# Which engine evicts the first transposed tile: a fixed choice in a planned FFT-convolution and GLU kernel

## The chip, the cores and the metric

The kernel runs on one core of one Trainium2 chip. The metric is the device time of one execution in microseconds; lower is better. Engines are named as in the profile: PE is TensorE, DVE is VectorE, ACT is ScalarE, POOL is GpSimd, SP is SyncE.

## The reference

The kernel computes the output and nine gradients of one block: a layer normalization, a gated long convolution of H3 type on one side, a gated linear unit on the other, and a residual sum. S is 2048, D is 512, F is 1376, everything is bf16.

```python
xn = _layernorm(x)                              # x = A_q
k_shift = sum(k_pad[:, t:t+S] * shift_k[:, 3-t] for t in range(4))
kv = k_shift * v
y = irfft(rfft(kv, 2*S) * rfft(ssm_k, 2*S))[:S] + kv * ssm_D
s = xn * y
g, u = xn @ w_gate, xn @ w_up
z = (sigmoid(g) * u) @ w_down
out = x + s * silu(z)
# returned: out, and the gradients for A_q, A_k, A_v, A_shift_k, A_ssm_k, A_ssm_D,
# B_w_gate, B_w_up, B_w_down against grad_out
```

## The kernel before

**Tiles.** The 2048 rows of the sequence are cut into 16 tiles of 128 rows. They are taken in the order `SEQ`, which begins with 15, 13, 11, 9, 7, 5, 0, 1, 2; `POS[i]` is the place of tile i in that order, so `POS[15]` is 0. The 512 channels are cut into four groups `cg` of 128 for the convolution.

**First part, to some 160 us.** Four streams are woven together. `strG` makes the forward half of the gated unit for nine tiles: `f_gen(i)` multiplies the transposed normalized tile `xnT` with `w_gate` and `w_up` in three chunks (`FBS`, of 4, 4 and 3 blocks of 128 columns), ScalarE makes the sigmoid of one half of the result, and VectorE multiplies the other half by it. `strK`, `strV` and `strX` make the long convolution as a transform by matmuls: `k_t` transposes the kernel of a channel group, `step1` is the first transform stage, `flip` a transpose, `step3` the second stage, `inv3` and `inv1` the way back. `strV` also has the four-tap shift as multiplies and adds of 128x2048 on VectorE. `gen_ci` transposes constants for the way back, and `gen_fft_consts` makes the transform's constants with sines on ScalarE right at the start. `w_gen`, early in the second part, transposes the last pieces of the weights.

**Second part.** From there `stepB` makes the down projection and the gradients tile by tile, `dW` the weight gradients, `frontC` and `backC` the gradients of the convolution.

**The transposed tile.** `f_ln` normalizes tile i into `xnA[:, i]`. `f_xt(i)` makes `xnT`. For the first four places of `SEQ`, and for places 9 to 11, it makes four TensorE transposes into a PSUM bank and evicts them with one copy of 128x512 in bf16; for the others a DMA transpose does it. `f_xt(15)` is called on its own ahead of the streams; `f_xt` of the next tile is called inside `f_gen`.

**What sets the order.** Nothing is issued where it is written. Every call is recorded by `Rec.add`, with its dependencies, and `Rec.order` then lays out all recorded operations on the five engines, from its own costs and due times: at each step it takes, over the engines, the operation that can start earliest, and among those that are ready on an engine the one that was recorded first. `Rec.emit` issues the result, which is why nearly all instructions of the profile have the line number 523. An operation waits on the chip only for what it needs, but each engine takes its instructions strictly in the planned order.

An eviction made with `nc.evac` is recorded with two alternatives, and the planner decides:

```python
def evac(self, dst, src, n):
    op = self.add([("scalar", "copy", (dst, src), {}), ("vector", "tensor_copy", (dst, src), {})])
    op.bias = 0.3 if esize(src.ap.dtype) == 2 else 0
```

In `order` such operations stand in the list `either`. VectorE gets one only when ScalarE would be late with it by more than 0.4 or 1.6 us of the planner's time, and bf16 evictions carry a bias of 0.3 towards VectorE. An operation recorded for one engine alone goes into that engine's own list.

PSUM has eight banks. A tile of PSUM is given its bank by the planner too. Results that need two banks (`mm2`: `f_gen`, `step1`, `step3`, `inv3`, `inv1` in the first part) take one of four pairs, of which the third is shared with `acc` (banks 4 and 5) and the fourth with `tr` (banks 6 and 7, where every transpose goes):

```python
KINDS = {"mm2": [(0, 1), (2, 3), (4, 5), (6, 7)], "mm2c": [(0, 1), (2, 3)], "mm1": [(0,), (1,), (2,), (3,)],
         "acc": [(4,), (5,)], "tr": [(6,), (7,)]}
```

DMAs are issued from SP (weights, k, v, half swaps of the transform, DMA transposes) and from POOL (x tiles after the third, stores to the scratch tensors `hF_d`, `sF_d`, `KK_d`, `ksh_d`).

Of the kernel before, what the change touches and what calls it, by code (L numbers as in the profile page):

```python
# [37 lines left out]
POS = {i: n for n, i in enumerate(SEQ)}  # L38
# [599 lines left out]
def kernel_impl(ctx, tc, A_q, A_k, A_v, A_shift_k, A_ssm_k, A_ssm_D, B_x, B_w_gate, B_w_up, B_w_down,  # L638
                grad_out, out_0, out_1, out_2, out_3, out_4, out_5, out_6, out_7, out_8, out_9):
    nc = tc.nc  # L640
# [24 lines left out]
    def ps_tr(shape, dt=bf16, name=None):  # L665
        return nc.ps("tr", shape, dt)
# [25 lines left out]
    T = [dict() for _ in range(NJ)]  # L692
# [31 lines left out]
    def f_xt(i):  # L724
        if POS[i] > 3 and not 8 < POS[i] < 12:
            T[i]["xnT"] = xnT_r.next()
            nc.sync.dma_start_transpose(T[i]["xnT"], xnA[:, i, :])
            return
        pt = ps_tr([4, 128], name="ps_xnT")
        for db in range(4):  # L730
            nc.tensor.transpose(pt[:, db, :], xnA[:, i, db * 128:(db + 1) * 128], ident)
        T[i]["xnT"] = xnT_r.next()
        nc.evac(T[i]["xnT"], pt[:], 512)

    def f_gen(i):
        xnT = T[i]["xnT"]
# [7 lines left out]
        for pi, (f0, nb) in enumerate(FBS):  # L744
            if PS["wide"]:
                ps = ps_mm([2, 4, 128], name="psGU")
                pg, pu = ps[:, 0], ps[:, 1]
            else:
                pg, pu = ps_mm([4, 128], name="psG")[:], ps_mm([4, 128], name="psU")[:]
            for pt_, w in ((pg, wg), (pu, wu)):  # L750
                for b in range(nb):
                    for db in range(4):
                        nc.tensor.matmul(pt_[:, b, :], w[:, db, (f0 + b) * 128:(f0 + b + 1) * 128], xnT[:, db, :],
                                         start=(db == 0), stop=(db == 3))
            nc.scalar.activation(sigT[:, f0:f0 + nb, :], pg[:, 0:nb, :], ACT.Sigmoid)
            if uT is None:
                nc.vector.tensor_tensor(hT[:, f0:f0 + nb, :], pu[:, 0:nb, :], sigT[:, f0:f0 + nb, :], ALU.mult)
            else:
                nc.evac(uT[:, f0:f0 + nb, :], pu[:, 0:nb, :], nb * 128)
            if pi == 1 and n + 2 < NJ:  # L760
                f_ln(SEQ[n + 2])
            if pi == (2 if n == 0 else 0) and n + 1 < NJ:
                f_xt(SEQ[n + 1])
            yield nb * 1024
# [101 lines left out]
    for db in range(4):  # L866
        pb = ps_acc([512])
        nc.tensor.matmul(pb[:], ones1, skr[:, db * 512:(db + 1) * 512], start=True, stop=True)
        nc.scalar.copy(skb[:, :, db * 128:(db + 1) * 128], pb[:].rearrange("p (d t) -> p t d", t=4))
    next(consts)  # L870
    f_xt(SEQ[0])
    f_ln(SEQ[1])
    next(consts)
# [668 lines left out]
```

## Time and profile before

| What | us |
|---|---|
| median of 6 runs | 515.98 |
| lowest and highest | 514.41, 519.02 |
| the profiled execution | 516.2 |
| its span, first to last instruction | 514.4 |
| PE busy | 494.6 (96%) |
| DVE busy | 387.1 (75%) |
| ACT busy | 349.8 (68%) |
| POOL busy | 129.3 (25%) |

A row of a timeline gives start, length, engine, line, operation, output and input, and how many instructions were merged into it; brackets hold the idle time before it and what ended that. A windows row gives, for a stretch, the busy time and the number of instructions of each engine, the granted TensorE clock, the busy share of the DMA engines and what they moved. A group row gives busy time, mean length in ns, and idle time with its releasers.

### The profile page before, as it was taken

How to read it: one execution, taken by the hardware profiler on the slowest of the kernel's cores; microseconds unless marked ns; L12 is line 12 of the kernel's file. 1: busy time of each engine (PE TensorE's matmuls, PEld its weight loads, DVE VectorE, ACT ScalarE, POOL GpSimd, SP SyncE). 2: the span in 40 equal slices, each digit the busy share in tenths (PEclk: the TensorE clock that was granted, in tenths of full speed). 3: DMA queues.
4: the chain of work that ended last, by engine and by line, in shares of the span. 5: the costliest groups of instructions: out<-in, count | busy, mean ns of one | idle time of the engine just before them, and what ended most of it. 6: DMA issues, size and time to landing. Idle time of an engine off the chain costs nothing.

```text
span 514.4 us, 13559 instructions
## 1 busy us (share of the span) xinstructions
PE 494.6 (96%) x5437; PEld 352.3 (68%) x5437; DVE 387.1 (75%) x772; ACT 349.8 (68%) x467; POOL 129.3 (25%) x251
## 2 busy tenths in 40 slices
PE   5699999999999999999999999999999999999997
PEld 3688897889886676666666556644675665866644
DVE  7688999986758789867779988426759859698440
ACT  6799999998874565465545546426878988886611
POOL 7243526255413333414153311000010010010000
PEclk9999999999999999999999999999999999999999
DMA  8989997599997555737499946989799699999973
GB/s 208 314 213 293 314 316 241 171 294 241 255 216 200 159 154 163 201 110 192 119 252 228 278 153 173 217 256 249 170 236 253 171 263 309 207 237 243 199 218 97
DMA packets 181392, 112.92 MB, mean 220 GB/s; under 512 B 131441, under 2 KB 165777, under 8 KB 181074
## 3 DMA queue, kind: packets, MB, share of 16 engines
q1 hardware_dynamic: 169376, 77.78, 64.2%
q0 software_dynamic: 11424, 34.29, 20.8%
q8 instruction: 42, 0.69, 0.6%
q14 instruction: 20, 0.16, 0.1%
q10 hardware_dynamic: 530, 0.01, 0.1%
HBM read 37.65 MB, written 45.72 MB: 162 GB/s over the span
## 4 chain that ended last, share of the span: by engine, by line
PE 79%; ACT 8%; DVE 6%; DMA 3%; issue 3%; POOL 1%; DVEq 0%; ACTq 0%; POOLq 0%; SPq 0%
PE psum L523 79%; ACT slab L523 8%; DVE slab L523 6%; DMA KK_d<-slab 1%; DMA slab<-in_A_ssm_D_dram 1%; DMA slab<-slab 1%; POOL slab L523 1%; DMA hF_d<-slab 0%; POOL hF_d L523 0%; POOL KK_d L523 0%; DVEq L523 0%; ACTq L523 0%; POOLq L523 0%; SPq L523 0%
## 5 line engine op out<-in xcount | busy, mean ns | idle before, releaser
L523 PE MATMUL psum<-slab 128*128 128x128 bf16 (+3 forms) x5437 | 494.6, 255 | 16.6 <-ACT slab L523 8.6
L523 PEld LDWEIGHTS <-slab 128*128 128x128 bf16 (+1 forms) x5437 | 352.3, 99 | 158.5 <-issue 13.9
L523 DVE TENSOR_TENSOR slab<-slab 128x512 bf16<-128x512 bf16 (+6 forms) x488 | 268.4, 600 | 49.9 <-ACT slab L523 42.2
L523 ACT CAST slab<-psum 128x1024 bf16<-128x1024 f32 (+5 forms) x278 | 224.3, 855 | 90.1 <-PE psum L523 79.1
L523 ACT ACTIVATE slab<-psum 128x512 bf16<-128x512 f32 (+2 forms) x80 | 53.9, 680 | 43.5 <-PE psum L523 40.3
L523 ACT ACTIVATE slab<-slab 128x512 bf16<-128x512 bf16 (+3 forms) x71 | 56.5, 809 | 14.6 <-DVE slab L523 13.9
L523 ACT COPY slab<-psum 128x1024 bf16<-128x1024 bf16 (+1 forms) x36 | 33.1, 950 | 11.7 <-PE psum L523 11.7
L523 POOL DMA_DIRECT2D out_dram<-slab x32 | 17.4, 545 | 93.8 <-DVE slab L523 93.8
L523 DVE TENSOR_TENSOR slab<-psum,slab 128x512 bf16<-128x512 f32 (+2 forms) x47 | 29.2, 624 | 13.0 <-ACT slab L523 10.4
L523 POOL DMA_DIRECT2D slab<-slab x8 | 4.3, 534 | 130.9 <-DVE slab L523 130.6
L523 POOL DMA_DIRECT2D hF_d<-slab x48 | 26.0, 543 | 36.2 <-DVE slab L523 34.7
L523 DVE SCALAR_TENSOR_TENSOR slab<-psum,slab 128x512 bf16<-128x512 f32 x16 | 11.0, 689 | 27.2 <-PE psum L523 27.2
L523 POOL DMA_DIRECT2D KK_d<-slab x32 | 17.5, 547 | 19.8 <-ACT slab L523 16.5
L523 DVE CAST slab<-psum 128x1024 bf16<-128x1024 f32 (+1 forms) x16 | 17.8, 1121 | 5.4 <-PE psum L523 5.3
L523 POOL DMA_DIRECT2D slab<-in_A_q_dram x29 | 16.3, 562 | 13.7 <-DVE slab L523 5.7
L523 DVE SCALAR_TENSOR_TENSOR slab<-slab 128x512 bf16<-128x512 bf16 (+3 forms) x41 | 16.9, 415 | 0.7
L523 DVE STREAM_TRANSPOSE slab<-slab 128x1024 f32<-128x1024 f32 x8 | 14.3, 1834 | 4.0 <-ACT slab L523 4.0
L523 DVE TENSOR_SCALAR slab<-slab 128x1 f32<-128x1 f32 (+9 forms) x48 | 12.0, 277 | 4.1 <-POOL slab L523 3.5
L523 DVE COPY slab<-psum 128x1024 bf16<-128x1024 bf16 (+1 forms) x21 | 13.0, 633 | 1.9 <-PE psum L523 1.9
L523 POOL DMA_DIRECT2D slab<-hF_d x18 | 9.7, 541 | 12.2 <-PE psum L523 10.1
L523 POOL TENSOR_TENSOR slab<-slab 128x1 f32<-128x1 f32 x16 | 10.2, 638 | 8.7 <-DVE slab L523 8.5
L523 DVE BATCH_NORM_STATS2 slab<-slab 128x6 f32<-128x512 bf16 x16 | 10.8, 682 | 0.1
(21 smaller groups left out, 40.8 us busy)
## 6 DMA issues: line engine op xcount, KB each, us to landing
KK_d<-slab POOLq DMA_DIRECT2D x32, 256.0 KB, 5.4
slab<-KK_d SPq DMA_DIRECT2D x16, 512.0 KB, 4.9
slab<-in_A_k_dram SPq DMA_DIRECT2D x8, 512.0 KB, 6.9
hF_d<-slab POOLq DMA_DIRECT2D x32, 128.0 KB, 4.0
slab<-slab SPq DMA_DIRECT2D x32, 128.0 KB, 4.9
out_dram<-slab POOLq DMA_DIRECT2D x32, 128.0 KB, 2.9
uF_d<-slab SPq DMA_DIRECT2D x32, 128.0 KB, 2.4
gF_d<-slab SPq DMA_DIRECT2D x32, 128.0 KB, 2.4
```

The costliest lines, as they stand in the source:

```text
L523: getattr(getattr(self.nc, eng), meth)(*[place(v) for v in a], **{x: place(v) for x, v in k.items()})
```

## The change

For the tile in the first place of `SEQ`, tile 15, the eviction of the transposed tile is recorded as a VectorE copy alone. For all others it stays a choice of the planner. The rest of the source is the same; the planner lays out the whole program again.

```diff
         T[i]["xnT"] = xnT_r.next()
-        nc.evac(T[i]["xnT"], pt[:], 512)
+        if POS[i] < 1:
+            nc.vector.tensor_copy(T[i]["xnT"], pt[:])
+        else:
+            nc.evac(T[i]["xnT"], pt[:], 512)
```

## The prediction

> **What bounds the kernel now.** I read the page's busy rows first, then the windows view by stage, then the timeline of the first 25 us, because the edit touches only the first tile.
>
> ```profile
> span 514.4 us, 13559 instructions
> PE 494.6 (96%) x5437; PEld 352.3 (68%) x5437; DVE 387.1 (75%) x772; ACT 349.8 (68%) x467; POOL 129.3 (25%) x251
> ```
>
> TensorE is busy for 96% of the span, so the time is the work of TensorE plus its holes. The windows view says where they are; columns are PE, PEld, DVE, ACT, POOL (busy us, instructions), granted clock, DMA share, GB/s:
>
> ```profile
> 0.00:20.00 20.00, 9.44 (x68) 6.81 (x69) 16.91 (x60) 15.65 (x23) 10.28 (x27) 1.00 0.96 257
> 30.00:110.00 80.00, 76.98 (x1185) 68.94 (x1183) 75.61 (x109) 77.54 (x95) 33.93 (x63) 1.00 0.87 259
> 110.00:160.00 50.00, 49.05 (x752) 43.74 (x751) 33.71 (x66) 40.39 (x56) 19.75 (x40) 1.00 1.11 248
> 160.00:350.00 190.00, 190.00 (x1721) 121.08 (x1719) 145.95 (x396) 96.12 (x159) 55.64 (x105) 1.00 0.70 190
> ```
>
> Four regimes: a start with TensorE half empty; 30 to 110 us with three engines near full, ScalarE fullest (2.5 us idle in 80, VectorE 4.4, TensorE 3.0); 110 to 160 us with room on both evicting engines; then TensorE without a hole. The start in detail, from the timeline (start, length, engine, work, and in brackets the idle time before it with its releaser):
>
> ```profile
> 13.79 0.61 PE L523 MATMUL psum<-slab 128*128 128x128 bf16 x4 [0.91 <-ACT slab L523]
> 15.29 1.01 PE L523 MATMUL psum<-slab 128*128 128x128 bf16 x8 [0.90 <-ACT slab L523]
> 19.23 18.68 PE L523 MATMUL psum<-slab 128*128 128x128 bf16 x248 [2.93 <-ACT slab L523]
> ...
> 14.23 1.92 ACT L523 CAST slab<-psum 128x1024 bf16<-128x1024 f32 x2
> 16.03 0.85 ACT L523 ACTIVATE slab<-slab 128x640 f32<-128x640 int32 x1
> 16.76 1.94 ACT L523 CAST slab<-psum 128x1024 bf16<-128x1024 f32 x2
> 18.55 1.11 ACT L523 COPY slab<-psum 128x512 bf16<-128x512 bf16 x2
> 19.69 1.28 ACT L523 ACT_TABLE_LOAD   x1
> ```
>
> The COPY x2 at 18.55 is the eviction of the transposed tiles 15 and 13. It stands behind four f32 evictions, and TensorE's first gate matmul (19.23) waits 2.93 us for it: this is the hole the edit aims at.
>
> **The change, part by part.** (1) *The copy.* Removed: one 128x512 bf16 copy on ScalarE. Added: one on VectorE. The instruction orders of both programs put it just before the normalization of tile 13, where VectorE waits for POOL:
>
> ```profile
> 10.07 0.60 DVE L523 TENSOR_SCALAR slab<-slab 128x1 int32<-128x1 int32 x4
> 11.37 0.41 DVE L523 TENSOR_SCALAR slab<-slab 128x512 bf16<-128x512 bf16 x1 [0.70 <-POOL slab L523]
> ...
> L523 DVE COPY slab<-psum 128x512 bf16<-128x512 bf16 x4 | 1.6, 416 | 0.6 <-PE psum L523 0.6
> L523 ACT COPY slab<-psum 128x512 bf16<-128x512 bf16 x9 | 5.3, 615 | 8.9 <-PE psum L523 8.9
> ```
>
> The transposes of tile 15 are matmuls 13 to 16 of the burst that, instruction by instruction, starts at 8.64 (0.107 us apart), so they end near 10.55. VectorE is free at 10.67; 0.416 us later, at 11.09, the tile is ready, inside the 0.70 us hole. Cost zero; without that cover 0.4 us on tile 13's normalization, which has nobody waiting before 17 us. [...] The rows say 0.416 against 0.615 us for this copy; I take the rows. [...]
>
> (2) *The first matmuls.* In the changed order the 32 matmuls of tile 15's first chunk stand ahead of the last step1 group. They need the copy (11.1), w_gate and w_up columns 0 to 511 (the DMA view: issued 6.82 and 8.82, 6.9 and 7.5 us to landing, so at most 16.3; both issues' own landings are 13.7 and 15.2), and a bank pair. With tiles 15 and 13 in the two transpose banks, the pair comes from the first f32 eviction, which ends near 15.2 and released the x8 at 15.29. So they start at 15.3 instead of 19.23: **3.9 us earlier**. The step1 group that loses this slot takes 0.9 us after them.
>
> (3) *The clock.* The windows 19.20:25.00 and 25.00:30.00 hold 55 and 85 matmuls: 0.105 us each, then 0.057, although the clock column says 1.00 in both.
>
> ```profile
> 19.20:25.00 5.80, 5.77 (x55) 5.76 (x55) 2.35 (x6) 2.80 (x4) 2.88 (x5) 1.00 1.17 289
> 25.00:30.00 5.00, 5.00 (x85) 4.76 (x83) 3.03 (x5) 3.26 (x5) 2.03 (x4) 1.00 0.93 233
> ```
>
> [...] TensorE is 3.9 - 0.4 = 3.5 us of work ahead by 25 us. If the rate instead changes at 25 us whatever precedes it, the 3.9 us are worth half: 1.9 us. I take 3.5. It decides nothing, as (4) shows.
>
> (4) *What is late next.* Walking the changed order with the rows' durations: VectorE multiplies tile 15's first chunk at 20.0, has tile 15 done at 26.9, and starts the 8 multiplies of strV (128x2048, 1.22 us each) at 27.4; the order puts all 8 in one block ahead of tile 13's second chunk. Before, the same 8 began at 28.20 and, split 5 and 3 around one psum multiply, ended at 38.5:
>
> ```profile
> 28.20 6.13 DVE L523 TENSOR_TENSOR slab<-slab 128x2048 bf16<-128x2048 bf16 x5
> 34.85 3.73 DVE L523 TENSOR_TENSOR slab<-slab 128x2048 bf16<-128x2048 bf16 x3
> 38.51 1.15 DVE L523 TENSOR_TENSOR slab<-psum,slab 128x512 bf16<-128x512 f32 x2
> ```
>
> The block ends at 27.4 + 9.8 = 37.2, a lead of 1.3 us. By then chunks of tiles 13 and 11 hold three bank pairs, and TensorE, done with what needs none near 35.5, waits for the evictions that end at 37.6 to 37.9. ScalarE has done 31.4 us of listed work by 38.6 against 39.4. The lead left at 39 us is therefore about **1.0 us** of the 3.5.
>
> (5) *The rest of the mix.* The planner chooses an engine for every other eviction anew, up to 160 us; behind that TensorE's order is unchanged. Counted by kind: ScalarE gains 6 bf16 evictions of 1024 (6 x 1.06), one of inv1 (1.05) and 2 weight pieces (2 x 0.62), and loses 5 f32 ones of step1 and step3 (5 x 1.05) and one tile copy net (0.62): +2.8 us. VectorE takes f32 (1.22) for bf16 (0.68): +0.4 us. Cumulated to the first matmul of tile 1 (111 us before) ScalarE has +5.2 us with TensorE 1.3 us further on; to that of tile 2 (122 us, TensorE equal) **+3.0 us**. Against this stands ScalarE's idle time, 2.5 us to 110 and some 1.5 to 122. It is idle where it waits for TensorE, so I count what TensorE is further on, 1.3 us; bounds: none of it, or 3.0.
>
> (6) *Queues.* The tile copy issues no DMA. With the tile, three hF stores and one sF store on POOL (0.54 us each to issue) and its next x load move about 3 us up, past KK_d stores; POOL is 42% busy there. On the DMA engines one more 128 KB store before 21.6 us costs the last weights 0.5 us at the measured 259 GB/s; TensorE asks for them near 24. SP's list is reordered only among half swaps, k, v and transposes from 25 us on. I bound this by -0.5 and +1.0 us and take 0.
>
> **Sum.** Against the profiled execution (516.2 us, span 514.4; median of the runs 515.98, so 0.2 above it): -1.0 + 3.0 - 1.3 + 0 = +0.7, so **516.9**. With all the idle time usable 515.2, with none 518.2; with (6) 514.7 to 519.2.
>
> **The rivals.**
> *Lead kept.* TensorE stays 3.9 us ahead. For it: from 160 us to 350 TensorE has no hole, so a lead there reaches the end whole, and 110 to 160 us has 9.6 us of ScalarE room. Against: 30 to 110 us has three full engines, and the lead is eaten where banks wait. Time: 516.2 - 3.9 = 512.3.
> *ScalarE becomes the bound of 30 to 110 us.* The place is the bf16 evictions of k_t and flip moved from VectorE (0.68) to ScalarE (1.06), and banks held meanwhile. It decides once ScalarE's extra work is more than the lead and usable idle time together: 5.2 at tile 1 against 1.0 + 1.3 already is; if the lead is gone and no idle helps, +5.2: 521.4. For it: 97% busy. Against: the surplus shrinks to 3.0 at tile 2 and 1.5 at tile 3.
> *The change does nothing.* Excluded: the order shows the copy on VectorE, and matmuls 53 to 1945 of 5437 in new places.
>
> **How the numbers follow.** Within 0.5% (2.6 us, about what a measurement of this kernel can tell from no change) lie 513.6 to 518.8. Lead eaten, 516.9: 0.40, of which 0.06 above 518.8. Lead kept, 512.3: 0.25, counted faster. ScalarE bound, 521.4: 0.35, slower. So faster 0.25, same 0.34, slower 0.41. The likeliest single case is the first, with its own range 514.7 to 519.2. The range takes most of both others: 511.5 to 523.
>
> **What would show it.** Right: a gate matmul near 15.3 us and no 2.9 us hole before it; matmuls 0.057 us apart from about 21 us; a TensorE hole near 36 to 38; ScalarE at 98% or more from 30 to 110; tile 2's first matmul near 123 us. Wrong: TensorE still 3 us ahead at 110 us (lead kept), or holes of over 8 us between 30 and 110 (ScalarE the bound); a difference that grows behind 160 us would be another cause altogether.

## The result, and the profile after

| Kernel | median us | lowest to highest | ratio to before | 95% interval |
|---|---|---|---|---|
| before | 516.2 (41 runs) | 514.13 to 520.01 | 1 | |
| after | 520.22 (20 runs) | 517.56 to 523.85 | 1.0078 | 1.006 to 1.0095 |

The changed kernel is slower by 4.0 us, 0.8%. Its profiled execution took 519.0 us with a span of 517.2, so it is 1.2 us faster than its median. The profiled execution of before was at its median. So the two traces differ by 2.8 us, the medians by 4.0; a second profile of each stands further down.

The page of the changed kernel, span and busy row:

```profile
span 517.2 us, 13569 instructions
PE 493.6 (95%) x5437; PEld 350.7 (68%) x5437; DVE 388.0 (75%) x769; ACT 353.0 (68%) x470; POOL 131.5 (25%) x251
```

TensorE has the same 5437 matmuls, and ScalarE 3.2 us more work. The windows view of the same run says where TensorE lost time (stretch, length, then busy us and instructions of PE, PEld, DVE, ACT, POOL, granted clock, DMA share, GB/s):

```profile
0.00:20.00 20.00, 12.56 (x113) 10.09 (x114) 17.64 (x60) 15.45 (x22) 9.59 (x25) 1.00 0.99 258
30.00:110.00 80.00, 72.26 (x1092) 63.83 (x1090) 72.45 (x102) 78.12 (x93) 34.77 (x60) 1.00 0.85 255
110.00:160.00 50.00, 49.44 (x760) 44.18 (x758) 34.13 (x63) 39.74 (x56) 19.29 (x38) 1.00 1.07 225
160.00:350.00 190.00, 187.47 (x1710) 119.73 (x1708) 144.59 (x396) 95.05 (x159) 55.71 (x105) 1.00 0.72 193
```

Against the rows of before: TensorE is 3.1 us busier in the first 20 us, 4.7 us less busy from 30 to 110 us, and 2.5 us less busy behind 160 us, where before had no hole at all. So the edit did what it says, and two other losses came with it.

The start, from the timeline (start, length, engine, line, operation, output and input, count; idle time before it and its releaser in brackets):

```profile
15.11 17.83 PE L523 MATMUL psum<-slab 128*128 128x128 bf16 x276 [0.90 <-ACT slab L523]
...
10.45 0.42 DVE L523 COPY slab<-psum 128x512 bf16<-128x512 bf16 x1
11.19 0.41 DVE L523 TENSOR_SCALAR slab<-slab 128x512 bf16<-128x512 bf16 x1 [0.31 <-POOL slab L523]
...
17.06 0.41 DVE L523 COPY slab<-psum 128x512 bf16<-128x512 bf16 x1
```

The copy runs at 10.45 for 0.42 us and delays nothing: the normalization behind it starts at 11.19, where before it started at 11.37. The gate matmuls begin at 15.11 instead of 19.23, and the hole of 2.93 us is gone. The copy at 17.06 is that of tile 13: in the new plan the planner gave this one to VectorE too, though the edit doesn't ask for it.

The waits of TensorE between 30 and 110 us (engine, output, line, what it waited for: us in total, times, longest), first before, then after:

```profile
PE psum L523 <- ACT slab L523: 1.8, 5, 0.7
PE psum L523 <- DVE slab L523: 0.6, 2, 0.4
```

```profile
PE psum L523 <- ACT slab L523: 6.4, 18, 0.8
PE psum L523 <- DVE slab L523: 1.1, 2, 0.7
```

This is the first loss: 18 short waits for evictions of ScalarE in place of 5, none over 0.8 us.

The second is one hole. The timeline of TensorE around 160 us, first before, then after:

```profile
149.79 22.39 PE L523 MATMUL psum<-slab 128*128 128x128 bf16 x272
```

```profile
149.79 13.76 PE L523 MATMUL psum<-slab 128*128 128x128 bf16 x189
166.08 6.11 PE L523 MATMUL psum<-slab 128*128 128x512 bf16 x35 [2.53 <-DVE slab L523]
```

The bracket names VectorE, but VectorE is not the engine that was late. The matmuls at 166.08 read the transposed `w_up`, which four DMA transposes on SP bring. The last of the four lands at 165.88 by the trace, 0.20 us before TensorE resumes. In before it lands at 159.0. SP's own timeline, first before, then after:

```profile
123.74 4.41 SPq L523 DMA_TRANSPOSE slab<-in_B_w_gate_dram  x2
...
131.59 9.49 SPq L523 DMA_TRANSPOSE slab<-in_B_w_down_dram  x3
141.14 6.30 SPq L523 DMA_TRANSPOSE slab<-in_B_w_gate_dram  x2
147.74 7.45 SPq L523 DMA_TRANSPOSE slab<-in_B_w_up_dram  x4
```

```profile
123.76 5.52 SPq L523 DMA_TRANSPOSE slab<-in_B_w_gate_dram  x2
130.09 2.10 SPq L523 DMA_TRANSPOSE slab<-in_B_w_down_dram  x1
132.88 13.30 SPq L523 DMA_TRANSPOSE slab<-in_B_w_down_dram  x3
146.23 7.15 SPq L523 DMA_TRANSPOSE slab<-in_B_w_gate_dram  x2
153.68 7.75 SPq L523 DMA_TRANSPOSE slab<-in_B_w_up_dram  x4
```

The first transposes go out at the same time, 123.7 us. Most of the delay arises in the three of `w_down`: SP is held for 13.3 us instead of 9.5. The second of `w_down` takes 12.9 us from issue to landing, against 9.0 before. Everything behind it on SP then moves back by 5 to 7 us, `w_up` last.

To put the two losses on one scale I summed, over all matmuls, the time between two starts beyond what the matmul itself takes at full rate (behind 30 us in before two starts are 0.056 us apart for 128 columns and 0.216 for 512, in the median). This counts holes and half-rate stretches alike; the first column includes the 5.6 to 5.9 us before the first matmul. Lost us, worked out from the instruction starts of each trace:

| Profiled run | 0 to 30 | 30 to 110 | 110 to 162 | 162 to 175 | span |
|---|---|---|---|---|---|
| before | 18.1 | 7.3 | 1.8 | 0.0 | 514.4 |
| before, second profile | 18.0 | 7.3 | 1.4 | 1.2 | 515.3 |
| after | 13.1 | 12.7 | 1.5 | 2.7 | 517.2 |
| after, second profile | 14.2 | 12.7 | 1.9 | 4.1 | 520.2 |

The edit earns 4 to 5 us in the first 30, loses 5.4 again by 110 us, and 1.5 to 4 more at 163 us.

### The profile page after: what moved, and what is told of

Same layout as the page of the kernel before. It is cut to its first block, busy times and chain, and to the rows that moved or that the text cites. A ratio compares the mean times of both kernels' runs of the same rounds, so it can differ in the third digit from the quotient of the medians.

```text
span 517.2 us, 13569 instructions
## 1 busy us (share of the span) xinstructions
PE 493.6 (95%) x5437; PEld 350.7 (68%) x5437; DVE 388.0 (75%) x769; ACT 353.0 (68%) x470; POOL 131.5 (25%) x251
## 4 chain that ended last, share of the span: by engine, by line
PE 74%; DVE 3%; ACT 3%; issue 2%; DVEq 0%; ACTq 0%
PE psum L523 74%; DVE slab L523 3%; ACT slab L523 3%; DVEq L523 0%; ACTq L523 0%
## 5 line engine op out<-in xcount | busy, mean ns | idle before, releaser
L523 PE MATMUL psum<-slab 128*128 128x128 bf16 (+3 forms) x5437 | 493.6, 255 | 20.4 <-ACT slab L523 10.2
L523 PEld LDWEIGHTS <-slab 128*128 128x128 bf16 (+1 forms) x5437 | 350.7, 99 | 163.0 <-DVE slab L523 16.2
L523 DVE TENSOR_TENSOR slab<-slab 128x512 bf16<-128x512 bf16 (+7 forms) x488 | 268.1, 600 | 51.5 <-ACT slab L523 40.8
L523 ACT CAST slab<-psum 128x1024 bf16<-128x1024 f32 (+4 forms) x274 | 221.5, 856 | 90.1 <-PE psum L523 79.4
L523 ACT ACTIVATE slab<-psum 128x512 bf16<-128x512 f32 (+2 forms) x80 | 54.7, 685 | 42.0 <-PE psum L523 38.7
L523 ACT ACTIVATE slab<-slab 128x512 bf16<-128x512 bf16 (+3 forms) x71 | 56.6, 809 | 15.0 <-DVE slab L523 13.9
L523 ACT COPY slab<-psum 128x1024 bf16<-128x1024 bf16 (+1 forms) x43 | 40.7, 982 | 12.4 <-PE psum L523 12.4
L523 POOL DMA_DIRECT2D out_dram<-slab x32 | 17.5, 545 | 96.2 <-DVE slab L523 96.2
L523 DVE TENSOR_TENSOR slab<-psum,slab 128x512 bf16<-128x512 f32 (+2 forms) x47 | 29.3, 627 | 12.5 <-ACT slab L523 6.7
L523 POOL DMA_DIRECT2D slab<-slab x8 | 4.3, 534 | 130.9 <-DVE slab L523 130.6
L523 DVE SCALAR_TENSOR_TENSOR slab<-psum,slab 128x512 bf16<-128x512 f32 x16 | 11.0, 690 | 29.6 <-PE psum L523 29.6
L523 POOL DMA_DIRECT2D hF_d<-slab x48 | 26.1, 545 | 21.2 <-DVE slab L523 20.3
L523 DVE CAST slab<-psum 128x1024 bf16<-128x1024 f32 (+1 forms) x20 | 22.6, 1140 | 3.8 <-PE psum L523 3.4
L523 POOL DMA_DIRECT2D KK_d<-slab x32 | 17.4, 544 | 24.0 <-ACT slab L523 18.3
L523 POOL DMA_DIRECT2D slab<-in_A_q_dram x29 | 16.2, 557 | 11.2 <-DMA out_dram<-slab 4.7
L523 DVE SCALAR_TENSOR_TENSOR slab<-slab 128x512 bf16<-128x512 bf16 (+3 forms) x41 | 16.9, 415 | 1.0 <-POOL slab L523 0.3
L523 DVE STREAM_TRANSPOSE slab<-slab 128x1024 f32<-128x1024 f32 x8 | 14.3, 1830 | 4.0 <-ACT slab L523 4.0
L523 POOL TENSOR_TENSOR slab<-slab 128x1 f32<-128x1 f32 x16 | 12.2, 761 | 10.3 <-DVE slab L523 10.2
L523 DVE TENSOR_SCALAR slab<-slab 128x1 f32<-128x1 f32 (+9 forms) x48 | 12.1, 277 | 2.1 <-POOL slab L523 1.6
L523 POOL DMA_DIRECT2D slab<-hF_d x18 | 9.7, 541 | 12.2 <-PE psum L523 10.1
L523 POOL DMA_DIRECT2D slab<-in_grad_out_dram x16 | 8.6, 540 | 12.4 <-DMA out_dram<-slab 7.9
L523 DVE COPY slab<-psum 128x1024 bf16<-128x1024 bf16 (+1 forms) x14 | 8.7, 629 | 3.8 <-PE psum L523 3.7
```

The costliest lines, as they stand in the source:

```text
L523: getattr(getattr(self.nc, eng), meth)(*[place(v) for v in a], **{x: place(v) for x, v in k.items()})
```

## The experiments

The two plans differ in the places of most matmuls from the 53rd to the 1945th. To separate the copy from the new plan, the experiments take a finished order, before's or after's, and move single recorded operations in it. `n` is the number under which an operation was recorded, `q` the alternative taken (1 is VectorE). These kernels are a few lines longer ahead of `emit`, so their profiles say L524 to L529 where the others say L523; it is the same line. The edits are shown shortened: `index of` stands for a search by `n`. Each ratio is to runs of before taken beside the kernel in question; the medians of before drift from 516.2 to 515.4 us between such groups, so kernels of different groups are compared by their ratios.

**1. The copy alone.** The order of before, with only tile 15's copy (n 76) moved to VectorE ahead of tile 13's normalization:

```diff
 seq = self.order()                # before's
+k = index of n == 76; op, q, *rest = seq.pop(k)
+k = index of n == 83; seq.insert(k + 1, (op, 1, *rest))
```

> The order of the kernel before is kept instruction for instruction; only the copy of tile 15 goes to VectorE, into the hole ahead of tile 13's normalization. Theory A (the copy is free and its lead is eaten between 30 and 110 us): first gate matmul near 16.3 us instead of 19.2, time 515 to 516, ratio 0.998 to 1.000. Theory B (lead kept): 513.3, ratio 0.995. Theory C (the copy itself costs): over 518, ratio 1.004 or more.

Measured: 513.56 us, ratio 0.9947 (0.9928 to 0.9966), faster by 2.7 us. Its timeline, and then its windows row of 30 to 110 us:

```profile
15.12 11.10 PE L527 MATMUL psum<-slab 128*128 128x128 bf16 x145 [0.90 <-ACT slab L527]
```

```profile
30.00:110.00 80.00, 76.66 (x1178) 68.44 (x1177) 75.59 (x110) 76.67 (x93) 34.47 (x63) 1.00 0.89 271
```

The same start at 15.1 as after, but from 30 to 110 us TensorE is busy 76.7 us as before, and its waits for ScalarE there stay at 1.6 us. A lead made at the start is therefore kept there when the rest of the plan stays: it is 3.7 us at the 500th matmul and 3.4 at the 1482nd (another 1.1 us goes near 138 us, where TensorE waits 1.7 us for VectorE). The edit by itself is a gain; what costs is the plan that the planner builds around it, 520.2 - 513.6 = 6.7 us.

**2. Without the `w_up` transposes.** After, with the four DMA transposes of `w_up` left out:

```diff
+seq = [e for e in self.order() if e[0].n not in (2421, 2422, 2423, 2424)]
```

> The order of the changed kernel, with the four DMA transposes of w_up (slab<-in_B_w_up_dram, 160 us) left out, so that part of the gradient's weights is missing. Theory W (the 2.5 us TensorE hole at 163.5 us is the landing of these transposes, and it is the loss): no hole there, time 516.5 to 517.5 against 520 of the changed kernel, ratio 1.001 to 1.003. Theory E (the loss is in the evictions chosen anew up to 160 us): still 519.5 to 520.5, ratio 1.007.

Measured: 518.72 us, ratio 1.0046 (1.0029 to 1.0062), against 520.48 for after, measured beside it. The hole at 163 us is gone (lost 0.0 from 162 to 175 us). So the hole is the landing of `w_up`, but only 1.8 us of the 4.2 go with it, fewer than the theory of the weights wanted. The trace of this kernel was 1.7 us behind before at 150 us already, and lost another 0.7 us in one wait at 290 us.

**3 and 4. Both kernels again**, unchanged, for a second profile of each.

> The changed kernel once more, for a second profile. Theory W: ratio 1.006 to 1.009 with a hole of 2 to 5 us near 163 us, ended by a weight transpose's landing, while TensorE stands at the same place as before at 150 us within 1 us. Theory E: a second profile is behind by over 2 us at 150 us already.

> The kernel before once more, for a second profile. Theory W: the last w_up transpose lands some 4 us before TensorE asks for it (159.0 against 163.5 in the first profile), no hole near 163 us. Theory E says nothing on it.

Measured: after 520.48 us, ratio 1.0076 (1.0054 to 1.0099), with a hole of 2.4 us ahead of the matmuls at 167.5 and 4.1 us lost there in all. The rest of the 4.1 is clock: behind the hole the matmuls of 512 columns start 0.427 us apart instead of 0.216, and the windows row of that stretch shows half the clock:

```profile
167.20:170.70 3.50, 3.18 (x8) 1.19 (x9) 1.52 (x4) 0.00 (x0) 2.14 (x4) 0.51 0.97 282
```

In the first profile of after the clock stayed at 1.00 behind the hole of 2.53 us. A mean granted clock of 0.997 or less, which is what one such stretch leaves by an estimate from this row (3.4 us at 0.51 in a span of 520.2), stands in 7 of 21 and 10 of 18 executions of after whose clock is on record, in 3 of 86 of before and in 1 of 17 of kernel 7 below. In after these are 1.8 to 1.9 us longer than the others in the mean.

Before took 517.04 us in its one run, with a hole of 1.0 us: the last `w_up` landed at 163.8. The expectation of no hole was missed. Before's `w_up` is on the edge too, in time in one execution and 1 us late in another. The second profile of after is also 1.7 us behind before at the 1960th matmul (150.55 against 148.84 us), where the first was 0.1 behind (148.96); that is more than theory W allowed and less than theory E asked. Its half-rate stretch at the start ended at 20.5 us instead of 18.3, and 1.2 of the 1.6 us between the two profiles are there at the 500th matmul already.

**5 and 6. Order and engines crossed.** Beside the copies of tiles 15 and 13, 37 evictions have another engine in after than in before. One kernel takes after's order, both copies on VectorE, with before's engines for the 37; the other takes before's order, with tile 15's copy alone on VectorE, and after's engines for them:

```diff
+swap = {...}                      # the 37 operations
+seq = [(op, 1 - q if op.n in swap else q, *rest) for op, q, *rest in self.order()]
```

> The changed kernel's order is kept, but the 37 other evictions whose engine the planner chose anew go back to the engine that they had before. Theory E1 (the evictions' engines cost the time between 30 and 110 us): TensorE's idle there falls from 12.7 to 7 to 8 us, time 515 to 516, ratio 0.998 to 1.000. Theory E2 (the order costs it, the engines do not): 12 to 14 us idle there, time 520, ratio 1.006 to 1.010.

> The mirror: the order of the kernel before with the copy alone on VectorE (513.6 us), and the 37 evictions on the engines that the changed kernel gives them. Theory E1: 518 to 520. Theory E2: 513 to 515.

Measured: 526.81 us, ratio 1.0213 (1.019 to 1.0236), and 525.05 us, ratio 1.0186 (1.0165 to 1.0207). The 30 to 110 rows, after's order first:

```profile
30.00:110.00 80.00, 67.94 (x992) 59.58 (x991) 66.49 (x94) 68.66 (x81) 28.94 (x51) 0.98 0.76 235
```

```profile
30.00:110.00 80.00, 69.32 (x1042) 61.14 (x1041) 65.91 (x91) 73.78 (x88) 29.26 (x54) 1.00 0.77 236
```

Both are worse than either whole plan, so neither theory holds: the 5 us between 30 and 110 us can't be put down to the engines alone or to the order alone. In the crossed kernels TensorE loses 19 and 16 us there while no evicting engine is above 93% busy. A likely reading, not tested singly, is that an eviction's place in the order suits only the engine it was planned on.

**7. `w_up` first.** After, with the second pair of `w_gate` transposes issued on SP behind the four of `w_up`:

```diff
+late = [e for e in seq if e[0].n in (2427, 2428)]
+seq = [e for e in seq if e[0].n not in (2427, 2428)]
+k = index of n == 2424; seq[k + 1:k + 1] = late
```

> The changed kernel with one move: the second pair of w_gate transposes is issued on SP behind the four of w_up. The gradient's first sum needs all of w_up at once, and w_gate 11 matmuls of 0.216 us, 2.4 us, later. Theory W (the hole near 164 us is the last weight's landing, in the order of the queue): the hole shrinks by about 2.4 us, time 517.5 to 518.5, ratio 1.003 to 1.004. Theory W' (the hole has another releaser): unchanged, 1.007.

Measured: 517.42 us, ratio 1.0034 (1.0022 to 1.0046). SP and TensorE in the timeline, and then the windows row behind 160 us:

```profile
144.77 10.07 SPq L527 DMA_TRANSPOSE slab<-in_B_w_up_dram  x4
154.89 3.83 SPq L527 DMA_TRANSPOSE slab<-in_B_w_gate_dram  x2
...
149.83 20.38 PE L527 MATMUL psum<-slab 128*128 128x128 bf16 x236
```

```profile
160.00:350.00 190.00, 190.00 (x1718) 120.93 (x1716) 145.91 (x396) 96.09 (x159) 55.43 (x105) 1.00 0.72 195
```

The hole is gone and TensorE is busy for all of the 190 us. Only two SP instructions were moved. By the ratios this is 1.0076 - 1.0034, or 2.2 us (2.3 with the 1.0078 of the result), give or take 1 us by their intervals. That is the price of the weights in after.

**8. Fewer stores beside the transposes.** Why does the landing take longer? The DMA view from 130 to 146 us (what, queue, count, KB each, median us from issue to landing), first before, then after:

```profile
KK_d<-slab POOLq DMA_DIRECT2D x4, 256.0 KB, 6.5
...
slab<-in_B_w_down_dram SPq DMA_TRANSPOSE x4, 7.7
```

```profile
KK_d<-slab POOLq DMA_DIRECT2D x4, 256.0 KB, 8.7
...
slab<-in_B_w_down_dram SPq DMA_TRANSPOSE x4, 9.7
```

As many stores, and each slower, as are the transposes: they may share something. The second profiles warn against reading more into this pair: there the stores take 8.9 us in before and 7.9 in after. What keeps the plans apart is the second `w_down` transpose, with 9.0 and 9.4 us in the two profiles of before, 12.9 and 11.4 in those of after. This kernel takes the eight `KK_d` stores of group 3 away from there, by issuing them behind a later operation (n 3158):

```diff
+ns = (1774, 1857, 1924, 2032, 2119, 2132, 2233, 2265)
+late = [e for e in seq if e[0].n in ns]; seq = [e for e in seq if e[0].n not in ns]
+k = index of n == 3158; seq[k + 1:k + 1] = late
```

> The changed kernel, with the eight KK_d stores of channel group 3 (256 KB each, on POOL between 116 and 140 us) issued behind the weights' transposes, so that they hold other data. Theory D (the w_down, w_gate and w_up transposes land late because they share the DMA engines with these stores): the second w_down transpose takes 9 us instead of 11 to 14, the last w_up lands by 161 us, no hole, time 517 to 518. Theory P (the transposes are late for a wait in the issuing queue): landing times as in the changed kernel, 520.

Measured: 526.54 us, ratio 1.0212 (1.0189 to 1.0234). The landings came as the sharing theory says:

```profile
130.05 5.98 SPq L527 DMA_TRANSPOSE slab<-in_B_w_down_dram  x3
141.22 7.57 SPq L527 DMA_TRANSPOSE slab<-in_B_w_up_dram  x4
```

SP is held 6.0 us for `w_down` instead of 13.3, its second transpose lands after 5.0 us instead of 12.9, the last `w_up` at 151.2, and there is no hole at 163 us. POOL's other transfers from 130 to 146 us land faster as well, in 4.2 to 4.6 us where they took 7.1 to 10.3 in the two profiles of after. The time was missed by 9 us, though: the eight stores, now on POOL from 199.84 us, come with a new TensorE hole of 8.4 us at 201. The landing is answered by this run, the time is not.

**9 and 10. The copy alone with `w_up` first, and before with `w_up` first.** The edits of 1 and 7 together, and that of 7 on before:

> The order of the kernel before, the copy of tile 15 on VectorE, and the second pair of w_gate transposes behind the four of w_up. Theory W (the weights' landing is on the edge in every order, as the second profile of the kernel before, with a 1.2 us hole at 162.6 us, says): 512.5 to 513.5, ratio 0.992 to 0.995, no hole near 160 us in any profile. Theory N (the copy alone already leaves the weights early enough, 155.7 against some 161): the same as the copy alone, 513.6, ratio 0.995.

> The kernel before with nothing but the second pair of w_gate transposes behind the four of w_up. Theory W: its runs lose 0 to 1.2 us at this place, so 515.3 to 516, ratio 0.998 to 1.000, and no hole. If the move itself is worth 3 us whatever the order: 513, ratio 0.994.

Measured: 512.38 us, ratio 0.9934 (0.9908 to 0.9959), last `w_up` at 150.0; and 515.35 us, ratio 0.9989 (0.9974 to 1.0004), no hole. With kernel 7 these make a row in which the weights are in time everywhere: before's plan 0.9989, the copy alone 0.9934, the new plan 1.0034. So the copy brings 2.8 us (2.97 by the two medians, which were measured side by side) and the new plan costs 5.2.

**11. A second copy.** Kernel 9 with tile 13's copy (n 290) on VectorE as well, placed behind the statistics of tile 11 (n 229):

> As the kernel before it in this call, and tile 13's copy goes to VectorE too, behind the statistics of tile 11. ScalarE then loads the sigmoid's table 0.6 us earlier. Theory A (ScalarE's list is the limit of 30 to 110 us): 0.4 to 0.6 us faster than that kernel, ratio 0.992. Theory B (TensorE has no hole there and nothing is won): the same within 0.3 us.

Measured: 511.86 us, ratio 0.9925 (0.9898 to 0.9953), the best here. It is 0.5 us below kernel 9, but the intervals overlap, so whether the second copy adds anything is open. TensorE's rate rose at 19.1 us, and from 30 to 110 us it is busy for 76.2 us, about as full as in the copy alone. So tile 13's copy on VectorE, which the new plan has too, is not by itself what costs there.

## Why the prediction was right or wrong

The difference of 4.0 us comes apart by the ratios above, times 516 us:

| Part | us | from |
|---|---|---|
| weights in time: new plan against old | +2.3 | 1.0034 - 0.9989 |
| weights late in after | +2.3 | 1.0078 - 1.0034 |
| less what they cost before | -0.6 | 1 - 0.9989 |
| sum | +4.0 | |

By the intervals the first two parts are each uncertain by about 1 us, and the third is not clear of zero. The traces, in the table of lost time, put the weights, less what they cost before, at 2.7 us (first pair of profiles) and 2.9 (second).

- **The copy and the first matmuls, (1) and (2): right.** It was forecast for 10.67 to 11.09 and ran at 10.45, at 0.42 us, at no cost. The matmuls were forecast for 15.3 and came at 15.11. The price was that of VectorE's row (0.416 us), not that of ScalarE's (0.615).
- **The clock, (3): right in kind.** The gate matmuls began at 15.11 us instead of 19.23, and the slow stretch ended earlier too. It was forecast to end near 21 us; it ended at 18.3 in one execution of after and 20.5 in the other, against 25.3 and 25.1 before. That the start of the burst sets its end was my estimate, and these ends don't show it.
- **The lead eaten, (4): right that it goes, wrong where.** The block of strV multiplies that I placed at 27.4 to 37.2 ran from 25.7 to 35.7, so it was early, and cost little. The gaps of TensorE about it:

```profile
33.38 1.10 PE L523 MATMUL psum<-slab 128*128 128x128 bf16 x16 [0.44 <-ACT slab L523]
...
35.08 0.38 PE L523 MATMUL psum<-slab 128*128 128x512 bf16 x1 [0.61 <-ACT slab L523]
36.00 2.20 PE L523 MATMUL psum<-slab 128*128 128x512 bf16 x27 [0.54 <-ACT slab L523]
```

  These sum to 1.6 us, for ScalarE. The 500th matmul is still 3.8 us ahead of before (47.64 against 51.45), the 1000th 1.9, and the 1500th is 0.8 behind. So the lead went piece by piece between 50 and 118 us, in the short waits for ScalarE that the waits view counts, and not in one place near 37. My lead at 39 us of 1.0 was wrong.
- **The eviction mix, (5): right in direction, too small.** The extra work of ScalarE was counted well: 2.8 us forecast, 3.2 measured (353.0 against 349.8 busy). What it costs TensorE was not. I set +3.0 and took back 1.3 for ScalarE's idle time; with the lead of 1.0 this made +0.7, bounds -1.0 and +2.0. Measured with the weights out of the way it is +2.3, at the upper bound within its uncertainty; the first profile of after showed +0.1 at 150 us, the second +1.7. ScalarE was 97.7% busy from 30 to 110 us (78.12 of 80), short of the 98% I asked for. Two readings were off from the start: in before the first matmul of tile 1 stands at 115.9 us and that of tile 2 at 126.7, not at the 111 and 122 on which the sum is built, and in after tile 2's came at 127.2, not 123. The rival in which ScalarE becomes the bound had the mechanism of this part, and its own mark was nearly met: holes of 7.7 us from 30 to 110, where it asked for over 8. That the rest is ScalarE's work rather than the order it is done in was not shown: the crossed kernels 5 and 6 don't separate the two, and the single waits were not isolated.
- **The queues, (6): the step that failed.** It reads "I bound this by -0.5 and +1.0 us and take 0". Measured is 2.7 and 2.9 us in the two pairs of profiles, outside the bound; by the ratios it is 1.7 us (+2.3 and -0.6 above), uncertain by more than 1 us. The step looked at what SP's list holds and at the first 30 us; it did not follow how long SP's DMA transposes for the second part take to land beside POOL's stores. In the first profiles SP issues the first of them at the same time as before, and all in the same order, but they land later, and those behind them go out later. The prediction rested on the row of 190.00 busy us from 160 to 350 us, and read "no hole" as "nothing late"; the second profile of before shows that this row was on the edge. It also had no term for the half clock that followed the hole in the second profile of after (0.51 for 3.4 us). It did say that "a difference that grows behind 160 us would be another cause altogether", and it was.
- **The outcome.** 520.2 lies in the range, and slower had the largest chance, but that owes something to luck. The likeliest case, 516.9, missed by 3.3: 1.6 in part (5) and 1.7 in part (6). And the chance of slower was put on ScalarE as the bound, which brought about half of what was measured; the weights, which brought the other half, stood in no case.

What stays open: which property of the new plan makes the second `w_down` transpose slow. It took 11.1 to 14.1 us in four profiles with after's plan (after twice, kernels 2 and 7) and 7.3 to 9.7 in six with before's order. Kernel 8 shows that the `KK_d` stores beside it delay it. It does not show which stores, nor why as many of them in the same 16 us hurt more in after.

## What to carry to other kernels

When a planner lays out the program, an edit has two effects, its own and that of the new plan; freeze the order and move only the edited operation before you judge the edit (here -2.7 us against +4.0). A row without a hole doesn't say by how much it has none: for every transfer that the next stage needs, take the margin from landing to first use, and count a move of that size as a possible loss. And where the engine that the profile names as releaser was not late, look for the DMA landing that coincides with the resumed instruction: here "<-DVE" was a DMA transpose.

## What the runs showed of the hardware

**One DMA transpose took more than twice as long beside stores of another queue.** The second `w_down` transpose took 12.9 and 11.4 us in the two profiles of after, and 5.0 in kernel 8, where eight stores of 256 KB are taken away from there. Most packets were not slower in after than in before: from 130 to 146 us the median packet took 18 ns (256 B, SP's queue) and 160 to 165 (4096 B, POOL's queue) in all four profiles of before and after. The means were higher and varied, 30 and 181 ns in the first profile of before, 37 and 281 in that of after, but 28 and 287 in the second of before. So some packets took far longer than the median, and these means don't tell the plans apart.

The busy share of the DMA engines was no measure of what they moved. In before it is higher (second number from the end) in the second of these stretches, where little more than half as much is moved (last number, GB/s):

```profile
140.00:145.00 5.00, 4.58 (x73) 4.24 (x74) 2.79 (x7) 3.43 (x6) 1.02 (x2) 1.00 1.17 323
145.00:150.00 5.00, 5.00 (x70) 4.05 (x68) 1.18 (x3) 3.65 (x6) 0.00 (x0) 1.00 1.31 178
```

**The half-rate start was not the same in two executions of one program.** From 15 to 20 us, the first profile of after and then the second:

```profile
15.00:20.00 5.00, 4.89 (x61) 4.89 (x61) 4.90 (x16) 4.60 (x7) 0.56 (x1) 1.00 1.13 331
```

```profile
15.00:20.00 5.00, 4.65 (x45) 4.65 (x45) 4.69 (x17) 4.08 (x6) 0.56 (x1) 1.00 1.14 334
```

Busy times are about equal, and the clock column says 1.00 in both, but one has 61 matmuls and the other 45. The stretch ended 2.2 us later in the second, which is worth 1.1 us of work at half rate, an estimate. The trace's clock record begins only where this stretch ends, at 18.29 and 20.48 us, so the column has nothing to show ahead of that, and the rate is to be read from the number of matmuls.

**Behind a hole of 2.4 us the clock was halved for 3.4 us, behind one of 2.5 us it was not.** In the second profile of after TensorE sat idle for 2.37 us ahead of 167.52 us; from 167.20 to 170.70 the granted clock was 0.51, and matmuls of 512 columns started 0.427 us apart instead of 0.216. In the first profile it sat idle for 2.53 us ahead of 166.08 us, and from there to 169.50 the clock was 1.00. So two holes of about the same length cost differently, 4.1 and 2.7 us in the table of lost time; what decides between them was not shown.
